# Sliding-window attention: the weighted sum by 32x32 identity tiles, a 128-row output projection, softmax as trees

## The chip, the core and the metric

The kernel runs on one core of one Trainium2 chip. The metric is the device time of one execution in microseconds. Beside the repeated time there is one profiled execution, whose trace lists every instruction of the core's engines: PE (TensorE matmuls; PEld are its weight loads), DVE (VectorE), ACT (ScalarE), POOL (GpSimd), and SP, which issues DMAs.

## The reference

Two independent halves are computed and joined along the last axis. Part B is a long convolution (a state-space kernel applied by FFT); the change leaves it alone. Part A is attention over a short dilated window:

```
S, D = 2048, 640;  H = 32 heads of Dh = 20;  W = 8 slots, dilation 2
q, k, v = split(x @ wqkv)
idx[s, w]    = s - 2 * w                      # masked where it is negative
logits[s, w] = q[s] . k[idx[s, w]] * Dh ** -0.5
attn         = softmax(logits over w)
o[s]         = sum over w of attn[s, w] * v[idx[s, w]]
out          = o @ wo
```

## The kernel before, in words

Part B takes the first two thirds of the time and ends in a loop of small matmuls into `ps_ib` (line 553). Part A follows: `partA_head` loads `x`, transposes it with identity matmuls to `xT` (L595) and projects the keys `kT` (L608). `partA` does the rest. All its PSUM tiles come from one pool of eight banks with the tag `bank`.

The 2048 positions are four segments (`sc`) of 512, and each segment is worked in two halves (`hf`) of 256. Logits, weights and values stand with 128 partitions = 4 segments x 32 heads, so that one DVE instruction serves all segments and heads at once. The free axes are then slot or dimension, and position.

- `proj_q_part` (L631) projects queries of one half; ACT copies them to `qT` (L632). `proj_v_part` (L640) projects one of the 20 dimensions of the values for all heads, by four column tiles of 32 (one for each segment); ACT copies to `v2` (L642), which has a halo of 14 positions, filled by one DMA.
- `logits_w(hf, w)`: DVE multiplies queries by shifted keys (L654, 5120 elements a partition), and PE sums the 20 products of each head by a matrix of ones (`Gs`, L657, 20 matmuls of 256 columns, column tiles of 32) into `ps_l`: 4 banks, two slots each.
- `softmax(hf)`: ACT copies the four banks to `lsb` in f32 (L664); in half 0 POOL masks the first positions (L667); DVE takes the maximum over the 8 slots by TENSOR_REDUCE on a permuted view (L669), subtracts it (L670); ACT takes Exp (L671); DVE sums by TENSOR_REDUCE (L673), takes the reciprocal (L674) and multiplies, to `attn` in bf16 (L676).
- `av_step(hf, dh, w)`: for ten of the 20 dimensions, DVE multiplies the shifted values by one slot's weights (L688, 2560 elements, tile `prod2`, two buffers), and PE adds the product to five banks `ps_o` by the 128x128 identity (L690, five matmuls of 512 columns). After slot 7 ACT copies the five banks to `o2` (L693). So PE is used only to sum over the slots.
- `out_proj(q)`: contracts over (head, dimension). Since a segment's 32 heads are 32 partitions, every matmul has 32 rows: 20 dimensions x 2 column halves x 4 segments, four row tiles side by side (L702, 160 matmuls of 320 columns), into all eight banks `ps_op`. ACT copies them to `ob` (L707, two buffers), and SP stores each `ob` (L709). `wo2` holds the output weights four times, once for each segment's partitions (L622, four DMAs).

The order is written out at the end of `partA`: logits of half 0 between the value projections; queries of half 1; softmax of half 0; logits of half 1; the 16 steps of half 0; softmax of half 1; `out_proj(0)` and `out_proj(1)` (both belong to half 0); the 16 steps of half 1; `out_proj(2)` and `out_proj(3)`. A scheduler then places the instructions on each engine: it puts the maximum of softmax 1 on DVE behind the fourteenth step of half 0, the rest of that softmax behind the sixteenth, and begins `out_proj` of finished dimensions between the last steps of its half on PE. On ACT the Exp of softmax 1 stands behind the ten copies of `ps_o` of half 0.

Of the kernel before, what the change touches and what calls it, by code (L numbers as in the profile page):

```python
# [612 lines left out]
def partA(tc, pools, psp, hd, A_wo, out_a, ident):  # L613
# [5 lines left out]
    wo2 = wp.tile([128, DH, D], bf16, name="wo2")  # L619
    wsrc = A_wo.rearrange("(h d) e -> h d e", d=DH)  # L620
    for sc in range(4):
        nc.sync.dma_start(out=wo2[32 * sc:32 * sc + 32], in_=wsrc)  # L622
# [21 lines left out]
    o2 = hp.tile([128, DH, 512], bf16, name="o2", tag="xn_o2")  # L644
    lps_all = {}
    at_all = {}
# [13 lines left out]
    def softmax(hf):  # L660
        lps = lps_all[hf]
        lsb = sp.tile([128, W, 256], f32, name="lsb", tag="lsb")
        for wp_ in range(4):
            nc.scalar.activation(out=lsb[:, 2 * wp_:2 * wp_ + 2, :], in_=lps[wp_][:], func=ACT.Copy, scale=SCALE)  # L664
        if hf == 0:
            for w in range(1, W):
                nc.gpsimd.memset(lsb[0:32, w, 0:DIL * w], -1e9)  # L667
        mx = sp.tile([128, 256], f32, name="mx", tag="mx")
        V.tensor_reduce(out=mx[:], in_=lsb[:].rearrange("p w s -> p s w"), axis=AX.X, op=A.max)  # L669
        V.tensor_tensor(out=lsb[:], in0=lsb[:], in1=mx[:].unsqueeze(1).to_broadcast([128, W, 256]), op=A.subtract)  # L670
        nc.scalar.activation(out=lsb[:], in_=lsb[:], func=ACT.Exp)  # L671
        sm = sp.tile([128, 256], f32, name="sm", tag="sm")
        V.tensor_reduce(out=sm[:], in_=lsb[:].rearrange("p w s -> p s w"), axis=AX.X, op=A.add)  # L673
        V.reciprocal(out=sm[:], in_=sm[:])  # L674
        at = sp.tile([128, W, 256], bf16, name="attn", tag="attn")
        V.tensor_tensor(out=at[:], in0=lsb[:], in1=sm[:].unsqueeze(1).to_broadcast([128, W, 256]), op=A.mult)  # L676
        at_all[hf] = at
# [3 lines left out]
    def av_step(hf, dh, w):  # L681
        at = at_all[hf]
        if w == 0:
            ops_all[(hf, dh)] = [psp.tile([128, 2, 256], f32, name="ps_o", tag="bank") for _ in range(5)]
        ops = ops_all[(hf, dh)]
        p2 = sp.tile([128, 10, 256], bf16, name="prod2", tag="prod2")
        off = HALO + 256 * hf - DIL * w
        V.tensor_tensor(out=p2[:], in0=v2[:, 10 * dh:10 * dh + 10, off:off + 256], in1=at[:, w, :].unsqueeze(1).to_broadcast([128, 10, 256]), op=A.mult)  # L688
        for b in range(5):
            MM(ops[b][:].rearrange("p a b -> p (a b)"), lhsT=ident[:], rhs=p2[:, 2 * b:2 * b + 2, :].rearrange("p a b -> p (a b)"), start=(w == 0), stop=(w == W - 1))  # L690
        if w == W - 1:
            for b in range(5):
                nc.scalar.copy(out=o2[:, 10 * dh + 2 * b:10 * dh + 2 * b + 2, 256 * hf:256 * hf + 256], in_=ops[b][:])  # L693

    def out_proj(q):
        pst = {}
        for sc in range(4):
            pst[sc] = [psp.tile([128, 320], f32, name="ps_op", tag="bank") for _ in range(2)]
        for d in range(DH):
            for eh in range(2):  # L700
                for sc in range(4):
                    MM(pst[sc][eh][:], lhsT=o2[32 * sc:32 * sc + 32, d, 128 * q:128 * q + 128], rhs=wo2[32 * sc:32 * sc + 32, d, 320 * eh:320 * eh + 320],  # L702
                       start=(d == 0), stop=(d == DH - 1), tile_position=(32 * sc, 0), skip_group_check=True)
# [22 lines left out]
    for (dh, w) in steps:  # L726
        av_step(0, dh, w)
# [78 lines left out]
```

## Time and profile before

| | |
|---|---|
| runs, median (lowest to highest) | 606.02 us (604.95 to 608.52), 3 runs |
| the profiled execution's own time | 604.23 us |
| its span, first to last instruction | 602.4 us |
| mean granted TensorE clock | 0.941 |
| busy: PE, DVE, ACT | 464.7 us (77%), 408.3 us (68%), 343.4 us (57%) |
| output weights: DMAs, KB each, median us to landing | 4, 800.0, 14.1 |
| output tiles `ob`: DMAs, KB each, median us to landing | 16, 160.0, 1.8 |

How to read the lines further down. A row of the table by stage gives the stretch in us from the span's start, its length, then busy time (and count of instructions) of PE, PEld, DVE, ACT and POOL, the clock granted to TensorE (1.00 is full), and what the DMAs did. A line of a group is: source line, engine, operation, output<-inputs, sizes, count | busy us, mean ns of one | idle us of the engine just before them and what ended it. In the list of waits, the numbers are us in total, how often, and the longest. A line of the timeline begins with start and length in us. A line of the chain of waits is a piece of the path that ended last: start, length, and what it was.

Matmuls overlap in PE's pipeline, so the mean duration of one (403 ns for L690) is longer than the distance of two. The distance is what a matmul costs in a row of its kind.

### The profile page before, as it was taken

The numbers are of one execution on the slowest core, as the hardware profiler recorded it, in microseconds if no ns is written. First come the engines' busy times: TensorE is split into PE (matmuls) and PEld (weight loads), VectorE is DVE, ScalarE is ACT, GpSimd is POOL, SyncE is SP. The second block draws the span as 40 slices with busy tenths as digits, with TensorE's granted clock in tenths as the row PEclk, the third lists the DMA queues.
The fourth block names the chain that finished last, engine by engine and source line by source line (L and its number), as shares of the span: only waits on it lengthen the run. The fifth ranks groups of instructions, "written<-read, shape, count | busy, mean of one in ns | idle before, by whom it ended". The sixth has DMA issues, their size and how long they took to land. (4 is left out here: it accounts for less than half of the span.)

```text
span 602.4 us, 15025 instructions
## 1 busy us (share of the span) xinstructions
PE 464.7 (77%) x6769; PEld 289.4 (48%) x6776; DVE 408.3 (68%) x468; ACT 343.4 (57%) x442; POOL 29.6 (5%) x41
## 2 busy tenths in 40 slices
PE   0034689897989889888988885799989736987984
PEld 0033357575655555464646575574468323334343
DVE  5458895979894978696669755260096798976920
ACT  2713898868698778958885844255535500123132
POOL 9100000100010001000000000000000000000000
PEclk9999999999999989997989997899989955989997
DMA  8965143115207003500520077889200000002001
GB/s 179 178 214 154 27 130 112 57 41 182 47 16 217 2 14 93 140 2 1 166 46 3 1 211 280 287 162 238 54 2 2 4 1 1 0 1 89 1 24 66
DMA packets 47060, 51.87 MB, mean 86 GB/s; under 512 B 36808, under 2 KB 43208, under 8 KB 43540
## 3 DMA queue, kind: packets, MB, share of 16 engines
q1 hardware_dynamic: 46196, 50.17, 30.6%
q8 instruction: 53, 0.87, 0.6%
q0 software_dynamic: 448, 0.74, 0.5%
q14 instruction: 11, 0.09, 0.1%
q10 hardware_dynamic: 352, 0.00, 0.0%
HBM read 33.71 MB, written 17.14 MB: 84 GB/s over the span
## 5 line engine op out<-in xcount | busy, mean ns | idle before, releaser
L654 DVE TENSOR_TENSOR prod<-qT,kT 128x5120 bf16<-128x5120 bf16 x16 | 44.3, 2821 | 34.3 <-ACT qT L632 31.0
L251 ACT ACTIVATE X<-ps_t 128x1024 bf16<-128x1024 int16 x60 | 60.7, 1042 | 7.4 <-PE ps_t L207 6.9
L251 ACT ACTIVATE Y<-ps_t 128x1024 bf16<-128x1024 int16 x60 | 60.1, 1046 | 3.0 <-PE ps_t L207 2.5
L289 PE MATMUL ps_k<-Y,X 128*32 128x64 bf16 x1280 | 57.1, 310 | 2.3 <-issue 1.1
L378 PE MATMUL ps_f<-BD,u 128*64 128x128 bf16 x320 | 22.8, 295 | 44.1 <-DMA BD<-c_BD 31.7
L341 DVE CAST A<-ps_f 128x1024 bf16<-128x1024 f32 x28 | 34.1, 1222 | 31.4 <-PE ps_f L378 31.0
L207 PE MATMUL ps_t<-RF,PF 128*128 128x512 f16 x160 | 48.7, 392 | 6.0 <-ACT Y L251 4.0
L292 PE MATMUL ps_k<-Y,X 64*32 64x64 bf16 x1280 | 49.6, 299 | 1.8 <-DVE Y L259 1.5
L688 DVE TENSOR_TENSOR prod<-v,attn 128x2560 bf16<-128x2560 bf16 x32 | 45.7, 1490 | 7.2 <-PE ps_o L690 7.1
L289 PEld LDWEIGHTS <-X 128*32 128x32 bf16 x1280 | 40.9, 148 | 20.1 <-issue 10.9
L690 PE MATMUL ps_o<-prod,ident 128*128 128x512 bf16 x155 | 42.8, 403 | 8.2 <-DVE prod L688 6.5
L292 PEld LDWEIGHTS <-X 64*32 64x32 bf16 x1280 | 36.9, 139 | 19.2 <-issue 16.7
L339 ACT CAST Ssp<-ps_f 128x1024 bf16<-128x1024 f32 x26 | 26.1, 1018 | 32.0 <-PE ps_f L389 31.9
L378 PEld LDWEIGHTS <-u 128*64 128x64 bf16 x320 | 20.8, 204 | 48.0 <-issue 47.9
L702 PE MATMUL ps_op<-wo,o 32*128 32x320 bf16 x640 | 36.2, 309 | 3.7 <-ACT ob L707 3.5
L257 DVE TENSOR_TENSOR Y<-Y,M 128x2048 bf16<-128x2048 bf16 x30 | 36.6, 1219 | 2.9 <-ACT Y L251 2.9
L259 DVE TENSOR_TENSOR Y<-Y,M 128x2048 bf16<-128x2048 bf16 x30 | 36.6, 1221 | 0.3
L263 DVE TENSOR_TENSOR X<-X,MX 128x2048 bf16<-128x2048 bf16 x30 | 36.6, 1219 | 0.1
L227 ACT ACTIVATE M<-ps_t 128x1024 bf16<-128x1024 f32 x30 | 30.1, 1025 | 9.7 <-PE ps_t L210 6.5
L693 ACT CAST o<-ps_o 128x512 bf16<-128x512 f32 x20 | 10.2, 605 | 42.6 <-PE ps_o L690 42.6
L657 PE MATMUL ps_l<-prod,Gs 128*32 128x256 bf16 x320 | 16.5, 352 | 21.8 <-DVE prod L654 21.8
L702 PEld LDWEIGHTS <-o 32*128 32x128 bf16 x640 | 21.3, 96 | 21.8 <-issue 17.1
(128 smaller groups left out, 830.0 us busy)
## 6 DMA issues: line engine op xcount, KB each, us to landing
Udram<-Ssp SPq DMA_DIRECT2D x5, 1024.0 KB, 4.2
U<-Udram SPq DMA_DIRECT2D x5, 1024.0 KB, 6.3
Uw<-Udram SPq DMA_DIRECT2D x10, 512.0 KB, 11.0
Zdram<-Z SPq DMA_DIRECT2D x4, 1024.0 KB, 8.6
Zall<-Zdram SPq DMA_DIRECT2D x4, 1024.0 KB, 15.3
wo<-in_A_wo_dram SPq DMA_DIRECT2D x4, 800.0 KB, 14.1
u<-in_B_u_dram SPq DMA_DIRECT2D x4, 640.0 KB, 12.1
xn<-in_A_x_dram SPq DMA_DIRECT2D x4, 640.0 KB, 6.6
```

What stands on the lines that cost most here:

```text
L207: MM(ps, lhsT=Pt[:, 2 * blk + th, 0:128], rhs=rhs, start=True, stop=True, skip_group_check=True)
L251: order(nc.scalar.activation(out=dst.rearrange("p a j t -> p a (j t)"), in_=ps[:].bitcast(i16)[:, :, 0::2], func=ACT.Sin, scale=SINSC))
L257: V.tensor_tensor(out=hi, in0=lo, in1=m(0), op=A.mult)
L259: V.tensor_tensor(out=lo, in0=lo, in1=m(2), op=A.mult)
L263: V.tensor_tensor(out=xf, in0=xf, in1=mx, op=A.mult)
L289: MM(o, lhsT=X[:, r, g, :, t], rhs=Y[:, r, g, :, t], start=(k == 0 and r == 0), stop=False, tile_position=(0, 32 * g), skip_group_check=True)
L292: MM(o, lhsT=X[hb:hb + 64, r, 4 + g % 2, :, t], rhs=Y[hb:hb + 64, r, 4 + g % 2, :, t], start=False, stop=(r == 1), tile_position=(hb, 32 * ...
L378: MM(ps[64 * r:64 * r + 64, i], lhsT=src_fn(8 * q + i), rhs=BD[:, r], start=(i % 4 == 0), stop=True, skip_group_check=True, tile_position= ...
L654: V.tensor_tensor(out=pr[:], in0=q4[:, :, :, 256 * hf:256 * hf + 256], in1=k4[:, :, :, 256 * hf:256 * hf + 256], op=A.mult)
L688: V.tensor_tensor(out=p2[:], in0=v2[:, 10 * dh:10 * dh + 10, off:off + 256], in1=at[:, w, :].unsqueeze(1).to_broadcast([128, 10, 256]), op ...
L690: MM(ops[b][:].rearrange("p a b -> p (a b)"), lhsT=ident[:], rhs=p2[:, 2 * b:2 * b + 2, :].rearrange("p a b -> p (a b)"), start=(w == 0), ...
L702: MM(pst[sc][eh][:], lhsT=o2[32 * sc:32 * sc + 32, d, 128 * q:128 * q + 128], rhs=wo2[32 * sc:32 * sc + 32, d, 320 * eh:320 * eh + 320], s ...
```

## The change

Three things are changed in part A, all in `partA`.

The softmax becomes a list of five steps. The maximum and the sum over the 8 slots are each made by three TENSOR_TENSOR instructions (8 to 4, 4 to 2, 2 to 1 slots) in place of one TENSOR_REDUCE. The steps of softmax 0 are written between the logits of half 1, and those of softmax 1 between the first eight steps of half 0.

The steps of the weighted sum take 8, 8 and 4 dimensions (`b`) in place of 10 and 10, so there are 24 a half. The sum over the slots is made by sixteen 32x32 tiles of the identity, one for each segment and each of four dimension groups (`dq`): the tile at row group `sc` and column group `dq` moves a segment's 32 heads to the output partitions of `dq`. Each segment has its own bank, in which the partitions are now 4 dimensions x 32 heads. `prod2` has three buffers of 2048 elements.

The output projection then contracts 128 partitions (4 dimensions x 32 heads) at a time: five matmuls of 128x128 by 320 columns for each bank (L723 of the changed kernel), two banks for 128 rows of output. `wo4` holds the weights once. The eight projections of half 0 are interleaved with the 24 steps of half 1; the eight of half 1 follow. The helper `interleave(a, b)`, which part B uses already, calls the functions of two lists in turn, in proportion to their lengths.

As the scheduler places it, the changed kernel has the whole of softmax 0 on DVE ahead of the eight products of the logits of half 1, as before. The instructions of softmax 1 stand on DVE between products of half 0, with two products between the subtraction and the first instruction of the sum; its Exp stands on ACT ahead of all copies of `ps_o`. On PE a projection of half 0 stands behind step 1 of half 1 and then behind every third step.

```diff
--- before.py
+++ after.py
@@ -616,10 +616,10 @@
     V = nc.vector
     wp, sp = pools["a_w"], pools["a_s"]
     hp, wsb, Gs, xT, kT = hd
-    wo2 = wp.tile([128, DH, D], bf16, name="wo2")
-    wsrc = A_wo.rearrange("(h d) e -> h d e", d=DH)
-    for sc in range(4):
-        nc.sync.dma_start(out=wo2[32 * sc:32 * sc + 32], in_=wsrc)
+    wo4 = wp.tile([128, 5, D], bf16, name="wo4")
+    wsrc = A_wo.rearrange("(h dd dq) e -> dq h dd e", dd=5, dq=4)
+    for dq in range(4):
+        nc.sync.dma_start(out=wo4[32 * dq:32 * dq + 32], in_=wsrc[dq])
     qT = wp.tile([128, 5, S], bf16, name="qT")
     x4 = xT[:].rearrange("p k (s i) -> p k s i", s=4)
     q4 = qT[:].rearrange("p c (s i) -> p c s i", s=4)
@@ -641,9 +641,8 @@
                    start=(kt == 0), stop=(kt == 4), tile_position=(0, 32 * sc), skip_group_check=True)
         nc.scalar.copy(out=v2[:, d, HALO:HALO + 512], in_=ps[:])
 
-    o2 = hp.tile([128, DH, 512], bf16, name="o2", tag="xn_o2")
+    o4 = hp.tile([128, 4, 5, 512], bf16, name="o4", tag="xn_o2")
     lps_all = {}
-    at_all = {}
 
     def logits_w(hf, w):
         if w == 0:
@@ -657,56 +656,74 @@
                 MM(lps[w // 2][32 * sc:32 * sc + 32, w % 2, :], lhsT=Gs[:, ct, :], rhs=pr[:, ct, sc, :],
                    start=(ct == 0 and w % 2 == 0), stop=(ct == 4), tile_position=(0, 32 * sc), skip_group_check=True)
 
-    def softmax(hf):
-        lps = lps_all[hf]
+    at_all = {}
+
+    def softmax_steps(hf):
+
         lsb = sp.tile([128, W, 256], f32, name="lsb", tag="lsb")
-        for wp_ in range(4):
-            nc.scalar.activation(out=lsb[:, 2 * wp_:2 * wp_ + 2, :], in_=lps[wp_][:], func=ACT.Copy, scale=SCALE)
-        if hf == 0:
-            for w in range(1, W):
-                nc.gpsimd.memset(lsb[0:32, w, 0:DIL * w], -1e9)
-        mx = sp.tile([128, 256], f32, name="mx", tag="mx")
-        V.tensor_reduce(out=mx[:], in_=lsb[:].rearrange("p w s -> p s w"), axis=AX.X, op=A.max)
-        V.tensor_tensor(out=lsb[:], in0=lsb[:], in1=mx[:].unsqueeze(1).to_broadcast([128, W, 256]), op=A.subtract)
-        nc.scalar.activation(out=lsb[:], in_=lsb[:], func=ACT.Exp)
-        sm = sp.tile([128, 256], f32, name="sm", tag="sm")
-        V.tensor_reduce(out=sm[:], in_=lsb[:].rearrange("p w s -> p s w"), axis=AX.X, op=A.add)
-        V.reciprocal(out=sm[:], in_=sm[:])
-        at = sp.tile([128, W, 256], bf16, name="attn", tag="attn")
-        V.tensor_tensor(out=at[:], in0=lsb[:], in1=sm[:].unsqueeze(1).to_broadcast([128, W, 256]), op=A.mult)
-        at_all[hf] = at
+        tr = sp.tile([128, 4, 256], f32, name="tree", tag="tree")
+
+        def fetch():
+            for wp_ in range(4):
+                nc.scalar.activation(out=lsb[:, 2 * wp_:2 * wp_ + 2, :], in_=lps_all[hf][wp_][:], func=ACT.Copy, scale=SCALE)
+            if hf == 0:
+                for w in range(1, W):
+                    nc.gpsimd.memset(lsb[0:32, w, 0:DIL * w], -1e9)
+
+        def tree(op):
+            V.tensor_tensor(out=tr[:], in0=lsb[:, 0:4], in1=lsb[:, 4:8], op=op)
+            V.tensor_tensor(out=tr[:, 0:2], in0=tr[:, 0:2], in1=tr[:, 2:4], op=op)
+            V.tensor_tensor(out=tr[:, 0], in0=tr[:, 0], in1=tr[:, 1], op=op)
+
+        def top():
+            tree(A.max)
+
+        def sub():
+            V.tensor_tensor(out=lsb[:], in0=lsb[:], in1=tr[:, 0].unsqueeze(1).to_broadcast([128, W, 256]), op=A.subtract)
+            nc.scalar.activation(out=lsb[:], in_=lsb[:], func=ACT.Exp)
+
+        def tot():
+            tree(A.add)
+            V.reciprocal(out=tr[:, 1], in_=tr[:, 0])
+
+        def norm():
+            at = sp.tile([128, W, 256], bf16, name="attn", tag="attn")
+            V.tensor_tensor(out=at[:], in0=lsb[:], in1=tr[:, 1].unsqueeze(1).to_broadcast([128, W, 256]), op=A.mult)
+            at_all[hf] = at
+        return [fetch, top, sub, tot, norm]
 
     ops_all = {}
 
-    def av_step(hf, dh, w):
+    def av_step(hf, b, w):
+
+
         at = at_all[hf]
+        nd = 8 if b < 2 else 4
         if w == 0:
-            ops_all[(hf, dh)] = [psp.tile([128, 2, 256], f32, name="ps_o", tag="bank") for _ in range(5)]
-        ops = ops_all[(hf, dh)]
-        p2 = sp.tile([128, 10, 256], bf16, name="prod2", tag="prod2")
+            ops_all[(hf, b)] = [psp.tile([128, nd // 4, 256], f32, name="ps_o", tag="bank") for _ in range(4)]
+        ops = ops_all[(hf, b)]
+        p2 = sp.tile([128, 8, 256], bf16, name="prod2", tag="prod2", bufs=3)
         off = HALO + 256 * hf - DIL * w
-        V.tensor_tensor(out=p2[:], in0=v2[:, 10 * dh:10 * dh + 10, off:off + 256], in1=at[:, w, :].unsqueeze(1).to_broadcast([128, 10, 256]), op=A.mult)
-        for b in range(5):
-            MM(ops[b][:].rearrange("p a b -> p (a b)"), lhsT=ident[:], rhs=p2[:, 2 * b:2 * b + 2, :].rearrange("p a b -> p (a b)"), start=(w == 0), stop=(w == W - 1))
+        V.tensor_tensor(out=p2[:, 0:nd], in0=v2[:, 8 * b:8 * b + nd, off:off + 256], in1=at[:, w, :].unsqueeze(1).to_broadcast([128, nd, 256]), op=A.mult)
+        for dq in range(4):
+            for sc in range(4):
+                sl = slice(32 * sc, 32 * sc + 32)
+                MM(ops[sc][32 * dq:32 * dq + 32], lhsT=ident[sl, sl], rhs=p2[sl, dq:nd:4], start=(w == 0), stop=(w == W - 1),
+                   tile_position=(32 * sc, 32 * dq), skip_group_check=True)
         if w == W - 1:
-            for b in range(5):
-                nc.scalar.copy(out=o2[:, 10 * dh + 2 * b:10 * dh + 2 * b + 2, 256 * hf:256 * hf + 256], in_=ops[b][:])
-
-    def out_proj(q):
-        pst = {}
-        for sc in range(4):
-            pst[sc] = [psp.tile([128, 320], f32, name="ps_op", tag="bank") for _ in range(2)]
-        for d in range(DH):
-            for eh in range(2):
-                for sc in range(4):
-                    MM(pst[sc][eh][:], lhsT=o2[32 * sc:32 * sc + 32, d, 128 * q:128 * q + 128], rhs=wo2[32 * sc:32 * sc + 32, d, 320 * eh:320 * eh + 320],
-                       start=(d == 0), stop=(d == DH - 1), tile_position=(32 * sc, 0), skip_group_check=True)
-        for sc in range(4):
-            ob = sp.tile([128, D], bf16, name="ob", tag="ob")
-            for eh in range(2):
-                nc.scalar.copy(out=ob[:, 320 * eh:320 * eh + 320], in_=pst[sc][eh][:])
-            st = 4 * sc + q
-            nc.sync.dma_start(out=out_a[128 * st:128 * st + 128, :], in_=ob[:])
+            for sc in range(4):
+                nc.scalar.copy(out=o4[:, sc, 2 * b:2 * b + nd // 4, 256 * hf:256 * hf + 256], in_=ops[sc][:])
+
+    def out_proj(hf, sc, q):
+        s0 = 256 * hf + 128 * q
+        ob = sp.tile([128, D], bf16, name="ob", tag="ob")
+        for eh in range(2):
+            ps = psp.tile([128, 320], f32, name="ps_op", tag="bank")
+            for dd in range(5):
+                MM(ps[:], lhsT=o4[:, sc, dd, s0:s0 + 128], rhs=wo4[:, dd, 320 * eh:320 * eh + 320], start=(dd == 0), stop=(dd == 4))
+            nc.scalar.copy(out=ob[:, 320 * eh:320 * eh + 320], in_=ps[:])
+        r0 = 512 * sc + s0
+        nc.sync.dma_start(out=out_a[r0:r0 + 128, :], in_=ob[:])
 
     for ct in range(5):
         proj_q_part(0, ct)
@@ -719,19 +736,24 @@
     nc.sync.dma_start(out=v2[32:128, :, 0:HALO], in_=v2[0:96, :, 512:512 + HALO])
     for ct in range(5):
         proj_q_part(1, ct)
-    softmax(0)
-    steps = [(dh, w) for dh in range(2) for w in range(W)]
+    sm = softmax_steps(0)
+    sm[0]()
+    sm = [None] + sm[1:]
     for w in range(W):
         logits_w(1, w)
-    for (dh, w) in steps:
-        av_step(0, dh, w)
-    softmax(1)
-    out_proj(0)
-    out_proj(1)
-    for (dh, w) in steps:
-        av_step(1, dh, w)
-    out_proj(2)
-    out_proj(3)
+        if w % 2 == 0:
+            sm[1 + w // 2]()
+    av = lambda hf: [(lambda b=b, w=w: av_step(hf, b, w)) for b in range(3) for w in range(W)]
+    sm = softmax_steps(1)
+    sm[0]()
+    for i, st in enumerate(av(0)):
+        st()
+        if i % 2 == 1 and i < 8:
+            sm[1 + i // 2]()
+    interleave(av(1), [(lambda sc=sc, q=q: out_proj(0, sc, q)) for sc in range(4) for q in range(2)])
+    for sc in range(4):
+        for q in range(2):
+            out_proj(1, sc, q)
 
 
 @with_exitstack
```

## The prediction

> **What bounds the kernel now.** The change touches the last third, so I read that part: first the table of engine times by stage, then the waits of DVE, then the groups by line.
>
> ```profile
> core 0: us, PE busy (x) PEld busy (x) DVE busy (x) ACT busy (x) POOL busy (x), PEclk, DMA share, GB/s
> ...
> 483.00:505.00 22.00, 8.82 (x144) 5.16 (x144) 22.00 (x10) 1.79 (x3) 0.00 (x0) 0.51 0.01 1
> 505.00:547.00 42.00, 35.86 (x292) 14.98 (x298) 36.20 (x22) 10.32 (x20) 0.00 (x0) 0.89 0.03 10
> 547.00:575.50 28.50, 24.93 (x222) 11.32 (x213) 22.78 (x16) 5.37 (x13) 0.00 (x0) 1.00 0.10 34
> 575.50:602.40 26.90, 17.43 (x311) 10.58 (x309) 0.00 (x0) 8.29 (x21) 0.00 (x0) 0.88 0.15 50
> ```
>
> The rows are: logits of half 1; weighted sum of half 0 with the softmax of half 1; weighted sum of half 1; the end. DVE is full in the first (22.00 of 22.00) and has holes in the next two. In the last 26.9 us it has no work: PE does half of the output projection there and ACT and the DMAs empty it. The waits of DVE from 455 us on name the holes:
>
> ```profile
> DVE sm L673 <- ACT lsb L671: 7.4, 2, 4.0
> DVE prod L688 <- PE ps_o L690: 7.1, 3, 5.5
> DVE mx L669 <- POOL lsb L667: 3.4, 1, 3.4
> ```
>
> The 5.5 us are the products of half 1 behind `out_proj(0)` and `out_proj(1)` in PE's queue; 4.0 of the 7.4 are the Exp of softmax 1, behind the copies of `ps_o` in ACT's queue. The groups that give the prices:
>
> ```profile
> L654 DVE TENSOR_TENSOR prod<-qT,kT 128x5120 bf16<-128x5120 bf16 x16 | 44.3, 2821 | 34.3 <-ACT qT L632 31.0
> ...
> L688 DVE TENSOR_TENSOR prod<-v,attn 128x2560 bf16<-128x2560 bf16 x32 | 45.7, 1490 | 7.2 <-PE ps_o L690 7.1
> ...
> L702 PE MATMUL ps_op<-wo,o 32*128 32x320 bf16 x640 | 36.2, 309 | 3.7 <-ACT ob L707 3.5
> ```
>
> **The change part by part** (against the profiled span, 602.4 us).
>
> *1. Softmax 0, on the path.* Two TENSOR_REDUCE give way to six f32 TENSOR_TENSOR of 1024, 512 and 256 elements.
>
> ```profile
> L669 DVE TENSOR_REDUCE mx<-lsb 128x256 f32<-128x2048 f32 x2 | 7.4, 3698 | 3.4 <-POOL lsb L667 3.4
> ...
> L670 DVE TENSOR_TENSOR lsb<-lsb,mx 128x2048 f32<-128x2048 f32 x2 | 4.6, 2290 | 0.0
> L88 DVE TENSOR_TENSOR cf_q<-cf_q 128x960 f32<-128x960 f32 x1 | 1.2, 1159 | 1.1 <-ACT cf_q L87 1.1
> ```
>
> 2.290 us at 2048 and 1.159 at 960 give 1.04 ns an element and 0.16 us fixed; so 1.22 + 0.69 + 0.43 and two gaps of 0.03 is 2.4 a tree, against 3.70 and 3.68. Two trees save 2.6 us. The chain of waits runs through mx and sm (softmax 0 lies between PE's last projection and the next products), so all of it counts. The waits for POOL and for Exp stay. The Trainium skill ("VectorE: DVE Perf Modes", section on the perf-mode tier table) speaks against this step: it gives tensor_reduce and fp32 tensor_tensor the same one element a cycle, by which 2048 elements in one instruction and 1792 in three would cost the same and the gain be nothing. The reduce's 3.70 us against 2.29 for as many elements contradicts that here.
>
> *2. Weighted sum, DVE side.* Per half 32 products' work is cut differently: 16 of 2560 elements become 16 of 2048 and 8 of 1024. Before, eleven in a row take 15.66 us, 1.42 each: 2560 elements at two a cycle by the slope of L654 and L688, (2821 − 1490)/2560 = 0.52 ns, is 1.33, and 0.09 is left. So 1.16 and 0.62: 16 × 1.16 + 8 × 0.62 = 23.5 us a half, against 16 × 1.42 = 22.8. It costs 0.7 twice.
>
> *3. Weighted sum, PE side.* Five 128×128 matmuls a step become sixteen 32×32 ones, each with its own weight load. No row shows sixteen tiles, one per position. The nearest: four column tiles with four different streams, in the timeline
>
> ```profile
> 456.63 2.35 PE L640 MATMUL ps_v<-xT,wsb 128*32 128x512 bf16 x40
> 458.79 0.74 PE L657 MATMUL ps_l<-prod,Gs 128*32 128x256 bf16 x20
> 459.34 1.03 PE L640 MATMUL ps_v<-xT,wsb 128*32 128x512 bf16 x13
> ```
>
> start to start 2.16/40 = 54 ns a matmul of 512 columns, a quarter of the 216 ns that the 128×128 form takes (50 L631 in 10.8 us): four at once, at no loss. Four row tiles into four banks (L702, 140 in 5.7 us) take 41 ns at 320 columns, where a quarter is 34. And 32×32 tiles on the diagonal, weight load included, with 160 columns:
>
> ```profile
> 392.05 0.52 PE ps_ib L553 x24
> ```
>
> 22 ns each. If row and column groups combine, sixteen take the larger of 216 and 16 × 22 = 0.35 us. If only four run at once it is 4 × 0.216 = 0.86 to 4 × 0.236 = 0.94 (0.43 to 0.59 at 256 columns). If two run at once, 1.73. I take 0.35: both directions are shown to overlap, each alone. Up to 0.86 it is under the product's 1.16, so in half 0 DVE sets the pace in either case. PE will be some 35% to 45% busy there, and the stage that is 40% busy now (483 to 505) has a clock of 0.51; at half clock 0.35 becomes 0.45 to 0.6, still covered.
>
> *4. Softmax 1 inside half 0's sum.* Its steps now stand between products on DVE: two products (2.3 us) cover the Exp (1.95 us), which no longer stands behind copies. DVE's 2.4 + 2.3 + 2.4 + 1.75 + 2.3 is 11.1; some gaps close, I take 10.7. The hole of 4.0 goes, and the 1.0 and 0.6 of the other two waits for PE, since three product buffers stand where two stood. Next late is DVE itself.
>
> *5. Half 1's sum with out_proj(0).* Eight projections of ten 128×128 matmuls of 320 columns: 10 × 0.136 = 1.36 us, by 216 ns at 512. Before, five L690 and two L702 take 1.43 where 5 × 0.216 + 2 × 0.04 is 1.16; the 0.26 are two changes of tile form, so 1.62 a projection. PE: 24 × 0.35 + 8 × 1.62 = 21.4 us against DVE's 23.5. Only in the eight short steps does PE bind: three projections and eight steps, 4.9 + 2.8 = 7.7, against 5.0; it ends about 2.5 us behind DVE. Added waits: a projection's first matmul needs a bank that ACT has emptied (0.4 us a copy), behind it stand three steps on PE, and behind those DVE's products; three buffers hold two steps, 2.3 us, so I cost it at nothing. If that cover fails it is up to 0.8 us, the longest such wait now, eight times: 6 us. ACT has some 12 us in these 23.5 (8 × 0.55 + 4 × 0.33 + 16 × 0.4). SP has only the eight output DMAs there.
>
> *Stage sum for 2 to 5.* Before, from the first product (504.85) to the last one's end (575.27): 70.4 us. After: 23.5 + 10.7 + 23.5 = 57.7. That is −12.7. PE may start half 1 at half clock (a projection at 2.7 us and three steps at 1.5 over 3.5 of DVE fills it, so it wakes within some 4 us): +1.
>
> *6. The end.* Before, 575.27 to 602.4 is 27.1 us: 2 × 160 matmuls, eight copies and DMAs each, all eight banks full before the first copy. After, only out_proj(1) remains. PE ends the steps 2.5 + 0.4 behind DVE; the first copy of `ps_o` 0.6; the first output tile 0.82 on PE and 0.45 copying. Then one tile per 1.4 us: PE 1.36; the two `ob` buffers 1.32, each 0.71 of copies, 1.84 to landing (DMA in the chain of waits) and 0.09. Seven more, 9.8. From the last copy to the end 3.1, as now (599.3 to 602.4). 2.9 + 0.6 + 0.82 + 0.45 + 9.8 + 3.1 = 17.7: −9.4.
>
> *7. Weights.* The DMAs of `wo` shrink from 800 to 200 KB each (14.1 us to landing, from 408 us on). Their first reader waits until 520 us and nobody stands behind them on SP before 467; nothing.
>
> Sum: −2.6 − 12.7 + 1 − 9.4 = −23.7 us. Span 578.7; with the 1.8 around it (604.23 − 602.4) 580.5 for the profiled run. That run is 1.8 below the median, 606.02; from the median it is **582.3 us**.
>
> **Rivals.**
>
> *A. The tiles run four at a time.* For it: L702's 41 ns where 34 would be ideal. Against: L640 loses nothing. Half 0 is unchanged; in half 1 PE has 16 × 0.94 + 8 × 0.59 + 13.0 = 32.8 us against 26.0 (DVE's 23.5 and the 2.5 behind): +6.8, **589 us**.
>
> *B. PE stays at half clock to the end.* For it: 0.51 in the logits, and gaps between steps. Against: the clock stands at 1.00 in 547 to 575.5, where PE is 87% busy. Half 1 on PE: 24 × 0.5 + 8 × 2.9 = 35.2, +9.2; the end 80 × 0.27 = 21.6 instead of 9.8 + 1.4, +10.4: **602 us**, about no change.
>
> *C. Slower: the sixteen tiles run one after another.* Each writes through a bank that four column groups share, so one could hold up the rest. At 216 ns each a long step is 3.46, a short one 1.76: 69.4 a half and 13 of projections, 152 us where I have 60: **674 us**. It decides from two at a time: at 108 ns a matmul half 0 takes 34.7 (DVE 34.2) and half 1 47.7, +22, which eats the gain. Against it speak the 54, 41 and 22 ns above.
>
> *D. The change doesn't do what it says:* the products would still wait for PE at each block's end, where four banks change hands. Two copies ahead of the first matmul, five times, 1.1 us each: +5.5, **588 us**.
>
> **Chances.** Forecast 0.66, A 0.13, D 0.11, B 0.05, C 0.05. The range reaches down by the 2.5 us behind DVE and the clock's 1, and some 4 us for copies and gaps that overlap better, to 575; up over D and A, and over a few us of clock, to 593: 575 to 593. A measurement of this kernel tells about 0.5% (3 us) from no change. Faster by more: forecast, A, D and a part of B, 0.91; within: most of B, 0.03; slower: C and what else, 0.06.
>
> **What would show it.** Right: DVE's group of products without waits for PE; six tree rows a half near 1.22, 0.69 and 0.43; sixteen matmuls starting within 0.35 to 0.6 us; no DVE hole over 1 us between the halves; 17 to 19 us from the last product to the end. Wrong: steps that start 0.9 us or more apart on PE with PE full (A); a clock of 0.5 in the last two stages (B); a matmul of the steps at 108 ns or more (C); waits of PE for ACT above 5 us in half 1 (D).

## The result, and the profile after

Four runs of the changed kernel have a median of **578.83 us** (576.19 to 580.98), four of the kernel before, taken beside them, 605.57 (604.95 to 608.52). The ratio is 0.9538, with a 95% interval of 0.9492 to 0.9583. The profiled run of the changed kernel took 579.84 us, its span is 578.1 at a mean granted clock of 0.914 (before 604.23, 602.4 and 0.941).

I cut each span at three marks: the first DVE instruction of softmax 0, the first product of the weighted sum, the end of the last product.

| us | span start to softmax 0 | to the first product | to the last product's end | to the end | softmax 0 to the end |
|---|---|---|---|---|---|
| before | 465.8 | 39.01 | 70.42 | 27.13 | 136.56 |
| after | 468.5 | 36.39 | 57.98 | 15.22 | 109.59 |
| difference | +2.7 | −2.62 | −12.44 | −11.91 | **−26.97** |

The first column holds code that the change does not touch, but for the smaller loads of the output weights. It lay between 464.2 and 470.6 in the profiles of this study, and between 464.2 and 468.5 in the three that have the changed kernel's own instructions. The last column repeats: these three (one of them has the sixteen matmuls of a step in another order) gave 109.59, 109.60 and 109.50. So I judge causes by the last column, which I call the tail, and not by the span: the two spans differ by 24.3 only because this profile of the changed kernel was 2.7 late before anything that the change touches. The medians differ by 26.7, near the tail's 27.0.

This is the table of engine times by stage of the kernel after: logits of half 1 with softmax 0; weighted sum of half 0 with softmax 1; weighted sum of half 1 with the first eight projections; the end. The columns are those of the table shown of before.

```profile
483.00:505.00 22.00, 8.82 (x140) 5.21 (x140) 22.00 (x10) 1.79 (x3) 0.00 (x0) 0.50 0.01 1
505.00:539.00 34.00, 15.20 (x404) 4.28 (x403) 34.00 (x34) 6.92 (x12) 0.00 (x0) 0.50 0.01 1
539.00:563.00 24.00, 21.03 (x431) 10.92 (x432) 22.36 (x24) 10.79 (x27) 0.00 (x0) 0.89 0.15 50
563.00:578.10 15.10, 11.74 (x115) 7.86 (x113) 0.00 (x0) 8.31 (x22) 0.00 (x0) 1.00 0.29 100
```

DVE is now full in the second row (34.00 of 34.00) and misses 1.64 us in the third. PE is 45% busy at half clock in the second row and 88% busy in the third, where the clock rises to full. The stage without DVE has shrunk from 26.9 to 15.1 us. The waits of DVE from 455 us on (us in total, times, longest) say which holes are left:

```profile
DVE tree L674 <- POOL lsb L671: 3.4, 1, 3.4
DVE tree L674 <- ACT lsb L683: 3.3, 1, 3.3
DVE prod L653 <- PE ps_l L656: 1.9, 2, 1.0
DVE prod L707 <- PE ps_o L711: 1.5, 3, 0.8
```

Of the two waits for Exp only that of softmax 0 is left (3.3, once); softmax 1 waits for nothing. The products wait 1.5 us for PE where they waited 7.1. The same view of PE:

```profile
PE ps_o L711 <- DVE prod L707: 21.7, 27, 2.7
PE ps_l L656 <- DVE prod L653: 15.5, 8, 5.2
```

PE waits for DVE alone, and in no row for ACT. The prices, from the groups of the window from 440 us to the end with different shapes kept apart:

```profile
L707 DVE TENSOR_TENSOR prod<-v,attn 128x2048 bf16<-128x2048 bf16 x32 | 37.2, 1215 | 0.8 <-PE ps_o L711 0.8
...
L707 DVE TENSOR_TENSOR prod<-v,attn 128x1024 bf16<-128x1024 bf16 x16 | 10.0, 683 | 0.7 <-PE ps_o L711 0.7
...
L674 DVE TENSOR_TENSOR tree<-lsb 128x1024 f32<-128x1024 f32 x4 | 4.9, 1221 | 6.7 <-POOL lsb L671 3.4 <-ACT lsb L683 3.3
L675 DVE TENSOR_TENSOR tree<-tree 128x512 f32<-128x512 f32 x4 | 2.7, 687 | 0.1
...
L676 DVE TENSOR_TENSOR tree<-tree 128x256 f32<-128x256 f32 x4 | 1.7, 421 | 0.1
```

A long product lasts 1.215 us, a short one 0.683, but neighbours overlap: start to start in a row they are 1.135 and 0.605 apart. The tree's three rows sum to 2.33 us a tree. PE's timeline shows the sums:

```profile
539.30 0.66 PE L711 MATMUL ps_o<-prod,ident 32*32 32x512 bf16 x16 [0.69 <-DVE prod L707]
539.90 2.85 PE L723 MATMUL ps_op<-wo,o 128*128 128x320 bf16 x10
...
557.21 0.44 PE L711 MATMUL ps_o<-prod,ident 32*32 32x512 bf16 x16 [0.70 <-DVE prod L707]
557.58 1.53 PE L723 MATMUL ps_op<-wo,o 128*128 128x320 bf16 x10
559.04 0.72 PE L711 MATMUL ps_o<-prod,ident 32*32 32x256 bf16 x48
559.69 1.53 PE L723 MATMUL ps_op<-wo,o 128*128 128x320 bf16 x10
...
563.27 0.44 PE L711 MATMUL ps_o<-prod,ident 32*32 32x256 bf16 x32
563.64 11.10 PE L723 MATMUL ps_op<-wo,o 128*128 128x320 bf16 x80
```

A step's sixteen matmuls take 0.66 us at half clock and 0.44 at full clock, to the last one's end. Three short steps, 48 matmuls, hold PE from 559.04 to 559.69: 0.65 us. A projection takes 2.85 at half clock and 1.46 start to start at full clock (557.58 to 559.04). The last eight projections follow without a break from 563.64 on, 0.8 us after the last product's end at 562.88. The chain of waits then alternates between copies and output DMAs; with two more output tiles (below) it stays on PE, and this part of the end is no shorter:

```profile
563.70 2.90 PE ps_op L723 x20
...
566.63 0.43 ACT ob L724
...
567.08 1.77 DMA out_dram<-ob
...
568.94 0.83 ACT ob L724 x2
...
569.79 1.78 DMA out_dram<-ob
```

### The profile page after: what moved, and what is told of

It is laid out like the page before. It is cut to its first block, busy times and chain, and to the rows that moved or that the text cites. A ratio compares the mean times of both kernels' runs of the same rounds, so it can differ in the third digit from the quotient of the medians.

```text
span 578.1 us, 15322 instructions
## 1 busy us (share of the span) xinstructions
PE 435.6 (75%) x6902; PEld 277.6 (48%) x6904; DVE 402.5 (70%) x492; ACT 345.4 (60%) x446; POOL 29.6 (5%) x41
## 5 line engine op out<-in xcount | busy, mean ns | idle before, releaser
L653 DVE TENSOR_TENSOR prod<-qT,kT 128x5120 bf16<-128x5120 bf16 x16 | 44.2, 2821 | 33.1 <-ACT qT L632 31.0
L707 DVE TENSOR_TENSOR prod<-v,attn 128x2048 bf16<-128x2048 bf16 (+1 forms) x48 | 47.0, 1038 | 1.5 <-PE ps_o L711 1.5
L711 PE MATMUL ps_o<-prod,ident 32*32 32x512 bf16 (+1 forms) x768 | 23.3, 458 | 21.7 <-DVE prod L707 21.7
L428 PE MATMUL ps_ia<-IA,U 128*128 128x128 bf16 x160 | 26.3, 245 | 5.9 <-DVE Z L341 2.6
L210 PE MATMUL ps_t<-RF,PF 128*64 128x512 f16 x160 | 25.6, 386 | 5.9 <-ACT X L251 3.9
L428 PE MATMUL ps_ia<-IA,Uw 128*128 128x128 bf16 x160 | 25.9, 245 | 2.0 <-DVE Uw L419 2.0
```

What stands on the lines that cost most here:

```text
L428: MM(ps[:, i], lhsT=p[:, :, :, 8 * q + i].rearrange("p g k -> p (g k)"), rhs=IA[:, r], start=(i % 4 == 0 and r == 0), stop=(r == 1), skip_ ...
L653: V.tensor_tensor(out=pr[:], in0=q4[:, :, :, 256 * hf:256 * hf + 256], in1=k4[:, :, :, 256 * hf:256 * hf + 256], op=A.mult)
L707: V.tensor_tensor(out=p2[:, 0:nd], in0=v2[:, 8 * b:8 * b + nd, off:off + 256], in1=at[:, w, :].unsqueeze(1).to_broadcast([128, nd, 256]), ...
```

## The experiments

**Theory T**, from the prediction: the change takes away four separate costs. The trees save DVE time; the softmax among the products removes the wait for Exp; the 32x32 tiles with the 128-row projection save PE time; the projections between the steps of half 1 use PE while DVE works. **Rivals:** the time comes from the new order alone and the tiles do nothing (R1), or from less PE work alone and the order does nothing (R2). Each part is undone by itself (the tiles and the form of the projection together), and one is done by itself. In the experiments the loss or gain is read from the tail.

### One part alone: the trees in the kernel before

```diff
-        V.tensor_reduce(out=mx[:], in_=lsb[:].rearrange("p w s -> p s w"), axis=AX.X, op=A.max)
+        tree(A.max)
...
-        V.tensor_reduce(out=sm[:], in_=lsb[:].rearrange("p w s -> p s w"), axis=AX.X, op=A.add)
+        tree(A.add)
```

> The kernel before with one edit: each TENSOR_REDUCE of the softmax is replaced by the three f32 TENSOR_TENSOR of the change. Theory: a tree is 1.3 us shorter than a reduction (3.70 against 2.4). Both trees of softmax 0 and the maximum of softmax 1 lie on the path; the sum of softmax 1 is followed by products that wait 5.5 us for PE's output projection, so its 1.3 us only lengthen that wait. 3 x 1.3 = 3.9: 601.7 us against 605.6. Rival 1, all four count: 600.4. Rival 2, the Trainium skill's equal rate of one element a cycle for both operations: 605.6, and tree rows that add up to 3.7 us.

Median 600.44 (598.10 to 601.53), ratio 0.9868 [0.9817, 0.992]. The tail is 133.01, −3.55: softmax 0 gives −2.61, the stretch of the products only −1.58, the end +0.64. The waits of DVE from 495 us on:

```profile
DVE prod L692 <- PE ps_o L694: 9.4, 3, 8.1
DVE tree L671 <- ACT lsb L676: 2.0, 1, 2.0
```

The longest wait for PE was 5.5 and is 8.1 now; the wait for Exp in softmax 1 was 4.0 and is 2.0. DVE comes out of softmax 1 earlier and stands that much longer behind the two projections in PE's queue. So of the 2.6 us by which softmax 1 is shorter, the products' stretch keeps 1.6 in the old order. The median fell by more than the tail, 7.7 us (600.4 is rival 1's figure, but from 605.6; here the kernel before ran at 608.09); the profiles show no cause for the rest in the part that the edit touches, and I count 3.55.

### The trees undone in the kernel after

```diff
-            V.tensor_tensor(out=tr[:], in0=lsb[:, 0:4], in1=lsb[:, 4:8], op=op)
-            V.tensor_tensor(out=tr[:, 0:2], in0=tr[:, 0:2], in1=tr[:, 2:4], op=op)
-            V.tensor_tensor(out=tr[:, 0], in0=tr[:, 0], in1=tr[:, 1], op=op)
+            V.tensor_reduce(out=tr[:, 0], in_=lsb[:].rearrange("p w s -> p s w"), axis=AX.X, op=op)
```

> The changed kernel with TENSOR_REDUCE put back in place of all four trees. Theory: DVE sets the pace from the softmax to the last product in the changed kernel, so all four count: 4 x 1.3 = +5.2, 584.0 us against 578.8. Rival, those of softmax 1 are hidden: +2.6, 581.4.

Median 582.85 (581.13 to 589.73), ratio 0.9628 [0.9573, 0.9682]; tail 115.18, +5.59. The group of the reduces:

```profile
L674 DVE TENSOR_REDUCE tree<-lsb 128x256 f32<-128x2048 f32 x4 | 14.6, 3655 | 6.7 <-POOL lsb L671 3.4 <-ACT lsb L681 3.3
```

Four times 3.66 is 14.6, four trees are 4.9 + 2.7 + 1.7 = 9.3: the difference, 5.3, is nearly all of what the tail shows. Whether the reduction itself is slow, or its reading through a permuted view, was not separated. In the new order all four trees are on the path, while the same trees in the old order gave 3.55.

### The projections of half 0 in one block

```diff
-    interleave(av(1), [(lambda sc=sc, q=q: out_proj(0, sc, q)) for sc in range(4) for q in range(2)])
+    for sc in range(4):
+        for q in range(2):
+            out_proj(0, sc, q)
+    for st in av(1):
+        st()
```

> The changed kernel with the eight output projections of half 0 in one block ahead of the steps of half 1 instead of between them. Theory: DVE runs three products ahead and then waits for the block: 8 x 1.36 us and some 2 us of half clock, less 3.4 ahead, 9 us of hole in DVE, and no projections left between the steps later: 588 us against 578.8. Rival, the interleaving only moves the wait into many small ones: 580 or less.

Median 587.35 (587.14 to 592.61), ratio 0.9687 [0.9617, 0.9757]; tail 119.84, +10.25. The waits of DVE:

```profile
DVE prod L707 <- PE ps_o L711: 10.2, 1, 10.2
```

One hole of 10.2 us: the products of half 1 fill their three buffers and stand behind 80 matmuls. R2 falls; where the projections stand is worth 10.25 us by itself, with the tiles unchanged.

### Softmax 1 in one block after half 0's steps

```diff
         st()
-        if i % 2 == 1 and i < 8:
-            sm[1 + i // 2]()
+    for k in range(1, 5):
+        sm[k]()
```

> The changed kernel with softmax 1 written in one block behind the 24 steps of half 0 instead of between its first eight. Theory: what the interleaving saves is the wait for Exp (2.0 us on ACT, perhaps behind the last copies of ps_o, up to 1.2 us more) and the small gaps between dependent instructions: +2.5 to +3.5, 581.8 us against 578.8. Rival, Exp is hidden anyway by the scheduler: 579.

Median 582.14 (580.59 to 583.36), ratio 0.9571 [0.9522, 0.962]; tail 112.25, +2.66. The second wait for Exp is back (5.4 in two, where it was 3.3 in one), and the rest are gaps that products had filled:

```profile
DVE tree L674 <- ACT lsb L683: 5.4, 2, 3.3
```

### The old tiles in the new order

The sum goes through the 128x128 identity again, and the projection through four row tiles of 32 rows, in four units between the steps; order and trees stay. `wo2` is back, and an output tile holds one column half (320 columns, four buffers).

```diff
-        for dq in range(4):
-            for sc in range(4):
-                MM(ops[sc][32 * dq:32 * dq + 32], lhsT=ident[sl, sl], rhs=p2[sl, dq:nd:4], ...)
+        for j in range(nd // 2):
+            MM(ops[j][...], lhsT=ident[:], rhs=p2[:, 2 * j:2 * j + 2, :], ...)
...
-    def out_proj(hf, sc, q):
+    def out_proj(hf, q, eh):
+        for d in range(DH):
+            for sc in range(4):
+                MM(pst[sc][:], lhsT=o2[32 * sc:32 * sc + 32, d, s0:s0 + 128], rhs=wo2[32 * sc:32 * sc + 32, d, 320 * eh:320 * eh + 320], ...)
```

> The changed kernel with its order, trees and steps of 8, 8 and 4 dimensions, but the old use of TensorE: 128x128 identity matmuls for the sum over slots (four or two a step), and the output projection by 32-row tiles into four banks, in units of one column half. Theory: the regrouping pays only because it empties PE. Half 0 stays with DVE; in half 1 PE has 16 x 0.86 + 8 x 0.43 + 4 units of 3.55 = 31.4 us against DVE's 23, +8; the end has four units of 3.3 and their copies instead of 11 us, +3: 590 us against 578.8. Rival 1, DVE sets the pace and the order alone did it: 579 to 581. Rival 2, the PE work itself was the gain: 600 or more.

Median 589.47 (587.92 to 590.69), ratio 0.9692 [0.9643, 0.974]; tail 119.62, +10.03: +7.3 in the products, +2.7 in the end. Its weighted sum of half 1, from the table by stage:

```profile
540.00:569.50 29.50, 29.32 (x399) 15.11 (x399) 22.35 (x23) 10.03 (x25) 0.00 (x0) 1.00 0.13 39
```

PE is busy for 29.32 of 29.50 us, DVE for 22.35. R1 falls: the order puts the projections into PE's idle time, and only the tiles make enough of it. PE's timeline says which of the two forms does that:

```profile
543.81 5.65 PE L709 MATMUL ps_o<-prod,ident 128*128 128x512 bf16 x24
549.39 2.90 PE L719 MATMUL ps_op<-wo,o 32*128 32x320 bf16 x80
```

Start to start, 24 matmuls of the 128x128 identity take 5.58 us, so the 80 of a half take 18.6; the 32x32 tiles take 5.8 (16 × 0.25 + 8 × 0.22, from the prices measured in this study). A unit of the projection takes 2.83 (the next row starts at 552.22), four of them 11.3; the eight 128-row projections take 8 × 1.46 = 11.7. So PE's time is saved in the sum over the slots, and the 128-row projection saves none of it against this form. The new form gives its output tiles one by one: from the start of PE's last long row of projections to the end it is 14.4 us in the kernel after and 17.2 here (570.22 to 587.4), with about 11 us of PE in both.

Undone one at a time, trees, projections, softmax and tiles cost 5.6 + 10.3 + 2.7 + 10.0 = 28.6 us, against 27.0 gained in all: the parts are not quite independent.

### The order of the sixteen tiles

```diff
-        for dq in range(4):
-            for sc in range(4):
+        for sc in range(4):
+            for dq in range(4):
```

> The changed kernel with the order of the sixteen matmuls of a step turned: four column groups of one row group (and bank) follow each other, instead of four row groups. Theory: all sixteen tiles are independent, so a step's sixteen keep their length (0.66 us at half clock, end of the last included) and the time stays at 578.8. Rival, tiles of one row group or one bank hold each other up: a longer step, 0.9 us or more.

One run, 575.54; tail 109.60, the same as the kernel after within 0.1 us, so the lower time lies in the unchanged part (464.2 us to softmax 0). Two steps of half 0 in the timeline:

```profile
501.93 0.65 PE L711 MATMUL ps_o<-prod,ident 32*32 32x512 bf16 x16
503.01 0.66 PE L711 MATMUL ps_o<-prod,ident 32*32 32x512 bf16 x16 [0.43 <-DVE prod L707]
```

At half clock the sixteen take the same 0.66 us, whether four neighbours in time share a row group or a column group. At full clock the 48 matmuls of three short steps again hold PE for 0.65 us (554.75 to 555.40).

### The sum three times

Each step issues its sixteen matmuls three times, so that the weighted sums come out tripled.

```diff
-        for dq in range(4):
+        for rp, dq in [(rp, dq) for rp in range(3) for dq in range(4)]:
```

> The changed kernel with every step's sixteen matmuls issued three times (the weighted sums come out tripled). It measures a set of sixteen by itself. Theory: sixteen tiles run together, 0.22 us a set of 512 columns at full clock; three sets take 0.7 and stay under the product's 1.14. Half 0 is unchanged, in half 1 PE has 24 x 0.6 + 8 x 1.8 = 28.8 us against 23.8: +5, 584 us. Rival A of the prediction, four at a time (0.86 a set): 2.6 a step, +70, about 650.

Median 600.75 (596.19 to 605.02), ratio 0.988 [0.9829, 0.9931]; tail 131.42, +21.8. The timeline of PE:

```profile
535.56 1.70 PE L711 MATMUL ps_o<-prod,ident 32*32 32x512 bf16 x128 [1.10 <-issue]
539.01 1.47 PE L711 MATMUL ps_o<-prod,ident 32*32 32x256 bf16 x128 [1.75 <-issue]
543.01 2.00 PE L711 MATMUL ps_o<-prod,ident 32*32 32x256 bf16 x128 [2.53 <-issue]
...
550.92 2.35 PE L711 MATMUL ps_o<-prod,ident 32*32 32x512 bf16 x144
553.20 1.53 PE L723 MATMUL ps_op<-wo,o 128*128 128x320 bf16 x10
```

The last two rows settle the price: 144 matmuls, nine sets, from 550.92 to the next matmul at 553.20, are 2.28 us, 0.25 a set and 16 ns a matmul with its weight load, the change to the projection's tile form included. The sixteen tiles run together: 16 × 216 ns one by one would be 3.46, four at a time 0.86. But the tail grew by 21.8 where the forecast had 5. The first three rows show why: PE stops each time after 128 matmuls, with their 128 weight loads 256 instructions, and the wait has the name "issue", in total

```profile
PE ps_o L711 <- issue: 10.7, 8, 2.5
```

From 535.56 to 539.01 and to 543.01 it is 3.5 and 4.0 us for 256 instructions, and the DMA rows of 534 to 548 us hold four packets of the queue that is named for instructions:

```profile
q8 instruction: 4, 0.07, 1.8%
```

0.07 MB in four packets is some 16 KB each, about one per stop. By the trace, packets of this queue begin at 533.26 (just ahead of that view), 536.63, 540.07 and 544.11 us and last 0.9 to 1.4 us, and 1.4 to 1.6 us after the end of each of them PE starts again: at 535.56, 539.01, 543.01 and 546.48. Of the 21.8 us, half 0 has 6.9, which the forecast took as unchanged; three of the stops lie there (1.10, 1.75 and 2.53). Half 1 has 12.2 and the end 2.7. There more stops, the added matmuls (by the set's price 16 × 0.50 + 8 × 0.44 = 11.5 us more on PE, which was 88% busy) and some 10 us at half clock come together, and their shares were not separated. Either PE runs out of instructions, or something in the long moving streams stops it.

### Twice more, but narrow

To tell these apart, the extra 32 matmuls of a step move only 32 columns, in seven slots of eight; 32 columns of the sums come out tripled. They cost hardly any streaming and as many instructions.

```diff
+        for rp, dq in [(rp, dq) for rp in range(2 if w < W - 1 else 0) for dq in range(4)]:
+            for sc in range(4):
+                MM(ops[sc][32 * dq:32 * dq + 32, 0, 0:32], lhsT=ident[sl, sl], rhs=p2[sl, dq, 0:32], start=False, stop=False, ...)
```

> The changed kernel with 32 more matmuls a step (in seven of eight slots), which move only 32 columns each (32 columns of the sums come out tripled). It has nearly the instruction count of the run with three full sets, at a fraction of its array time. Theory: PE stalled there for its instructions, which come in blocks of 256 (128 pairs of weight load and matmul) every 3.5 to 4 us; then this run is about as slow, 127 to 131 us from softmax 0 to the end, with stalls after every 128 matmuls. Rival, the array time of the sets cost it: 110 to 112 us.

One run, 592.50; tail 122.60, +13.0. The timeline of PE:

```profile
549.55 0.84 PE L728 MATMUL ps_op<-wo,o 128*128 128x320 bf16 x5 [1.71 <-issue]
550.32 0.43 PE L711 MATMUL ps_o<-prod,ident 32*32 32x512 bf16 x16
550.54 0.49 PE L716 MATMUL ps_o<-prod,ident 32*32 32x32 bf16 x32
550.86 0.51 PE L711 MATMUL ps_o<-prod,ident 32*32 32x512 bf16 x16
551.09 0.49 PE L716 MATMUL ps_o<-prod,ident 32*32 32x32 bf16 x32
551.40 0.51 PE L711 MATMUL ps_o<-prod,ident 32*32 32x512 bf16 x16
551.63 0.26 PE L716 MATMUL ps_o<-prod,ident 32*32 32x32 bf16 x11
553.28 0.26 PE L716 MATMUL ps_o<-prod,ident 32*32 32x32 bf16 x21 [1.37 <-issue]
```

Between the two stops stand 5 + 16 + 32 + 16 + 32 + 16 + 11 = 128 matmuls again, in the middle of a step and with tiles and widths mixed. The count decides, not the streaming. The packets of the instruction queue agree: two end at 548.05 and 551.93 us, and PE goes on 1.5 and 1.4 us later. The waits of PE in this kernel from 455 us on have three rows of that name:

```profile
PE ps_o L716 <- issue: 7.9, 6, 2.0
PE ps_o L711 <- issue: 1.8, 2, 1.2
PE ps_op L728 <- issue: 1.7, 1, 1.7
```

That is 11.4 us of stops beside a tail 13.0 longer. The narrow matmuls are not free either: 32 of them hold PE for 0.32 us (550.54 to 550.86), 10 ns each, more than a full set of sixteen. The theory's tail, 127 to 131, was too high in size; 122.6 is still far from the 110 to 112 of the rival.

### Quarters, and more buffers

If the end is 14.4 us of projections of a half, a weighted sum by quarters of 128 positions should leave only four of them for the end. The steps become 16 and 4 dims of 128 positions, and each quarter's four projections follow the long steps 0, 2, 4 and 6 of the next.

```diff
-    def av_step(hf, b, w):
-        nd = 8 if b < 2 else 4
+    def av_step(hf, q, b, w):
+        nd = 16 if b == 0 else 4
...
+    with_proj(0, 1, 0, 0)
+    with_proj(1, 0, 0, 1)
+    with_proj(1, 1, 1, 0)
     for sc in range(4):
-        for q in range(2):
-            out_proj(1, sc, q)
+        out_proj(1, sc, 1)
```

> A version meant to be faster: the weighted sum goes by quarters of 128 positions (steps of 16 and 4 dimensions, so that a long product still has 2048 elements), and the projections of each quarter stand between the long steps of the next one. Only four projections are left at the end. Theory: the end loses 4 x 1.36 = 5.4 us, DVE gains 8 short products a half, about +0.5 each half, and PE's slack in half 0 takes the projections at no cost: 574.3 us against 578.8. Rival, the end is paced by the output tiles' copies and DMAs and PE falls behind in half 0 at half clock: 577 to 579.

Median 579.32 (574.29 to 580.99), ratio 0.9523 [0.9486, 0.956]; tail 108.54, −1.05. The end did shrink by 6.0 (9.21 us), but the products stretch grew by 5, so the time came out as the rival had it. DVE's and PE's rows:

```profile
DVE prod L706 <- PE ps_o L710: 5.0, 7, 0.9
```

```profile
544.38 0.66 PE L710 MATMUL ps_o<-prod,ident 32*32 32x512 bf16 x16 [0.86 <-ACT o L714]
544.98 2.71 PE L722 MATMUL ps_op<-wo,o 128*128 128x320 bf16 x10
```

At the last two changes of quarter PE waits 0.86 us for ACT's copies, and at all three it then runs a projection at half clock (2.7 to 2.9 us long instead of 1.53); three product buffers do not cover that. So six product buffers and four output tiles were given to the quarters and, as a companion, to the kernel after, with the kernel after itself once more beside them:

```diff
-        p2 = sp.tile([128, 16, 128], bf16, name="prod2", tag="prod2", bufs=3)
+        p2 = sp.tile([128, 16, 128], bf16, name="prod2", tag="prod2", bufs=6)
...
-        ob = sp.tile([128, D], bf16, name="ob", tag="ob")
+        ob = sp.tile([128, D], bf16, name="ob", tag="ob", bufs=4)
```

> The version by quarters with six product buffers instead of three and four output tiles instead of two. In the version by quarters DVE waited 5.0 us for PE, behind projections at half clock and behind banks and output tiles that ACT had not emptied. Theory: more buffers let DVE run on over these, so most of the 5.0 goes: the stretch from softmax 0 to the end falls from 108.5 to 105 us, against 109.6 of the changed kernel; 574 us where the changed kernel has 579. Rival, the waits for the four banks at each change of quarter stay and PE falls asleep as before: 108.

> The changed kernel with the same buffers and nothing else. Theory: DVE waits 1.5 us for PE in it, of which the buffers can take no more than that, and the end is paced by PE: 108 to 109.6 us from softmax 0 to the end, 578 us. Rival, the two output tiles pace the end: up to 2 us less there.

> The changed kernel once more, as the companion of the version by quarters in one call. All theories: 109.6 us from softmax 0 to the end; the time as before, about 579, with what the unchanged part does by itself.

| | median us (range) | ratio to before [95%] | to the last product's end | end | tail |
|---|---|---|---|---|---|
| kernel after again | 577.65 (575.19–580.43) | 0.9481 [0.9437, 0.9526] | 57.98 | 15.13 | 109.50 |
| with the buffers | 579.54 (575.52–581.87) | 0.9510 [0.9444, 0.9576] | 56.2 | 16.1 | 108.67 |
| quarters with the buffers | 574.78 (571.35–578.47) | 0.9436 [0.9385, 0.9486] | 59.1 | 9.5 | 105.07 |

The quarters' remaining wait is small:

```profile
DVE prod L706 <- PE ps_o L710: 1.7, 2, 1.4
```

The buffers alone take the last 1.5 us of waits from DVE and give half of it back at the end, which PE paces, not the output tiles: from the start of PE's last 80 matmuls to the end it is 14.4 us with two output tiles and with four (563.64 to 578.1, 561.97 to 576.4). With the quarters the buffers are worth 3.5 us, since the waits that they cover are there; which of the two kinds does it there was not separated. Quarters with buffers have the lowest median and tail, 4.4 us under the kernel after's tail; the intervals of the ratios overlap, so the tail and not the total carries that.

## Why the prediction was right, step by step

The forecast sum was −23.7 us against the profiled span and the tail shows −26.97. That the forecast span, 578.7, stands so close to the measured 578.1 is partly luck: 2.7 us of late start in the untouched part made up for most of the 3.3 by which the sum was short. The forecast for the median, 582.3, is 3.5 us above the measured 578.83.

1. **Softmax 0**: forecast −2.6, measured −2.62; the tree rows are 1.22, 0.69 and 0.42 against 1.22, 0.69 and 0.43. The Trainium skill ("VectorE: DVE Perf Modes", section on the perf-mode tier table) gives tensor_reduce and fp32 tensor_tensor the same one element a cycle; undoing the trees costs 5.59 us, so the measurement decides against it here.
2. **Products**: 1.16 and 0.62 forecast, 1.135 and 0.605 start to start measured: 16 × 1.135 + 8 × 0.605 = 23.0 us a half instead of 23.5.
3. **The sixteen matmuls**: forecast 0.35 (0.45 to 0.6 at half clock), measured 0.25, and 0.43 at half clock (in the tripled run 48 in a row end after 1.51 us where sixteen alone end after 0.66). Rows and columns do combine. The 22 ns of L553, which I took as the price of a 32x32 matmul with its load, was no floor: here it is 16.
4. **Softmax 1 among products**: the holes went as said. Half 0 with softmax 1 took 33.1 us from first product to first product of half 1 (forecast 23.5 + 10.7 = 34.2).
5. **Half 1**: 24.85 us (forecast 23.5 and 1 for the clock): 23.0 of products, 1.5 of waits for PE, 0.3 of gaps. The half clock held until about 544 us, 6 us into half 1 where some 4 were forecast; the longest of the waits (0.8) stands behind the projection at half clock, the other two behind projections among the short steps. The copies of ACT that might hold a projection up, costed at nothing, cost nothing: PE has no wait for ACT.
6. **The end**: forecast 17.7 (17 to 19 among the signs of being right), measured 15.2. **This is the term of the sum that was mis-sized**: PE was to end the steps 2.9 us behind DVE and was 0.8 behind. I had 7.7 us of PE against 5.0 of DVE in the eight short steps, with 0.35 for each short set and 1.62 a projection; the runs show 0.22 (0.65 / 3) and 1.46, so 3 × 1.46 + 8 × 0.22 = 6.1 against 8 × 0.605 = 4.8. The rest, 14.8 forecast, was 14.4; one output tile per 1.36 us (11.10 / 8 = 1.39 on PE) was right.
7. **Weights**: nothing was seen of them on the path, as said.

Of the rivals, A (four tiles at a time, 0.86 us a set) falls by the 0.25, and C (one or two at a time) by the same row. B held for half 0 and 6 us of half 1; PE then filled up and had 1.00. D falls: the blocks' ends cost DVE no visible wait but the 1.5 in all.

That the trees, the order and the tiles each matter was argued in the prediction and is shown by the four experiments that undo them. What it did not say is how they need each other: the old tiles in the new order leave PE with 29.3 us of work in a stage where DVE has 22.4, and of what the trees of softmax 1 saved in the old order, part was given back at the next wait for PE. Theory T also counts the 128-row projection among what saves PE time; beside the form of the experiment the saving lies in the sum over the slots alone.

Not settled: why the untouched part varies by 6 us between executions. In 350 to 400 us the granted clock was 0.90 in the profile of before and 0.83 in that of after; no experiment was made on that. Whether three product buffers rather than two matter in the new order, or steps of 8, 8 and 4 dimensions rather than 10 and 10, was not tried.

## What to carry to other kernels

Where two engines alternate, put the second's spare work (here a projection) between the steps of the first, and make the steps' own share small enough that both fit: with either one undone, some 10 of the 27 us were lost again. Price a change on the stretch that it touches, marked at an instruction that both traces have; the total carried 6 us of variation from code that nobody had changed, the stretch 0.1. A saving ahead of a wait for another engine is only worth what that engine lets through: the same trees were worth 3.6 us in one order and 5.6 in the other.

## What the runs showed of the hardware that was not expected

- Sixteen 32x32 tiles, four rows by four columns, ran at 16 ns a matmul with its weight load (512 columns, full clock) and 27 ns at half clock; 48 of 256 columns took 0.65 us, 13.6 ns each, in either order of the tiles; 32 of 32 columns took 0.32 us, 10 ns each.
- PE's instructions came in blocks of 256 (a packet of 16 KB each), one per 3.5 to 4.0 us at most. A stage that used them up faster stopped for up to 2.5 us under the name "issue" (10.7 us in total with the sum tripled) and went on 1.4 to 1.6 us after the next packet's end. The kernel after stays below: 24 × 16 + 80 matmuls with their loads, 928 instructions in the 25 us of half 1, are a block per 7 us.
- PE had a granted clock of 0.50 from 483 to 539 us, busy in short bursts for 40% and 45% of the time; then the projections filled it (4.70 of 5.00 us busy in 539 to 544, still at 0.50), and from 544 on it had 0.99 to 1.00.
- A reduce of 2048 f32 elements through a permuted view took 3.66 us, a tensor_tensor of as many, read in order, 2.29.
